# Row- and column-tiled matmuls and one list schedule for all engines, in a kernel of memory-recurrent attention and a SwiGLU layer

## The chip, the cores and the metric

One core of one Trainium2 chip. The metric is the device time of one execution in microseconds (us); several runs were taken of each kernel that is compared closely. Runs carry a state: "fast" if they lie within 1.5% of the fastest of the same kernel; a single run is "unknown".

## The reference

```python
def _A_ref(x, mem0, Wq, Wk, Wv, Wo, seg_len):        # x: 2048 x 576, 32 heads of 128, 8 memory rows
    mask = (idx[:, None] < M) | (idx[:, None] >= idx[None, :])
    mem = mem0
    for s in range(n_seg):                           # 64 segments of 32 rows, one after the other
        h = jnp.concatenate([mem, xs], axis=1)       # 40 rows
        q, k, v = ...                                # three einsums of h with Wq, Wk, Wv
        p = _softmax(where(mask, q k^T * scale, -1e9))
        o = einsum('bhte,hed->btd', p v, Wo)
        mem = o[:, :M, :].copy()                     # the recurrence
        outs.append(o[:, M:, :])
# _B_ref: (silu(x w1) * (x w3)) w2 with 4608 inner columns; everything bf16
x = x + _A_ref(_layernorm(x), ...);  x = x + _B_ref(_layernorm(x), ...)
x = x + _A_ref(_layernorm(x), ...);  x = x + _B_ref(_layernorm(x), ...)   # the same weights
```

Cut: the random inputs, the batch dimension of 1. The model width of 576 is 4.5 times 128, and 9 times 64; this is what the change turns on.

## The kernel before

72 steps. In step t, layer 1 handles segment t and layer 2 segment t - 8, side by side as 2 x 40 columns. Steps 8 to 63 hold both layers, the first and last eight steps one. Four steps share one FFN job (128 rows of each layer that has some); jobs 0, 1, 16 and 17 hold one entry, the others two. All matmuls of Q, K and V contract over 128 rows in five passes, where the fifth holds the last 64 rows of Wq or Wv in one half and those of Wk (or of the other half of Wv) in the other, and meets zeros in the half that it doesn't use:

```python
for kind in range(2):                                    # Q, then K
    accv = acc[:, 0:hg * 2 * QW]...
    Wm, tailc = (WQ, 4) if kind == 0 else (WK, 5)
    for hl in range(hg):                                 # 6 or 4 heads
        for c in range(4):
            mm(accv[:, hl], lhsT=Wm[:, c, hh * E:(hh + 1) * E], rhs=ht_cols(c), ...)      # 128 x 128 weights, 80 columns
        mm(accv[:, hl], lhsT=T1[:, hh * E:(hh + 1) * E], rhs=ht_cols(tailc), ...)
    nc.scalar.activation(QKT[...], acc..., ACT.Copy)     # all Q/K copies on ScalarE
...
for c in range(4):                                       # V: HT is the stationary operand, 512 columns of Wv stream
    mm(acc[0:104, 0:a1 - a0], lhsT=HTt[:, c, :], rhs=WV[:, c, a0:a1], ...)
...
for gu, tailc in ((0, 4), (1, 5)):                       # FFN up: w1, then w3
    for c in range(4):
        mm(accv[:, gu, lo:hi], lhsT=W13M[:, wss[gu], c, fb * P:(fb + 1) * P], rhs=XTB[:, c, lo:hi], ...)
    mm(accv[:, gu, lo:hi], lhsT=W13T[:, wt, fb * P:(fb + 1) * P], rhs=XTB[:, tailc, lo:hi], ...)
```

The order of the work is fixed by hand: slots within a step, rings of buffers. Cut: softmax, output projection, layernorm, FFN down.

## Time and profile before

| kernel before | |
|---|---|
| time, first three runs | 3563.51 us (3555.35 to 3567.45) |
| TensorE / VectorE / ScalarE busy | 93% / 54% / 46% |
| matmuls, with a weight load each | 58,470 |
| one step in the middle (steps 12 to 63) | 50.1 us |

The prediction shows the page's main lines, the stages and a stretch of the timeline. Two lines that it did not show turn out to matter. The first is of the table of DMA queues (queue and kind: packets, MB, share of the 16 engines):

```profile
q8 instruction: 458, 7.50, 0.9%
```

I take queue 8 for the one that brings TensorE's own program: it has 458 packets of 16,384 bytes. The page counts 58,470 matmuls and as many weight loads; their sum divided by 458 packets is 255 (256 in the kernel after, with 725 packets), so my estimate from these counts is that a packet holds 256 instructions of 64 bytes. At 0.9% of the DMA engines it looks negligible. The second is a window, the first 60 us of the kernel before, in which the attention weights load (columns as in the stage table of the prediction):

```profile
0.00:60.00 60.00, 18.87 (x246) 15.73 (x246) 13.87 (x39) 8.23 (x15) 11.38 (x20) 0.83 1.06 336
```

### The profile page before, as it was taken

To read this page: it belongs to the slowest core of one execution; us is meant where nothing else is said; L and a number is where in the kernel's file an instruction comes from. 1 tells how busy PE (TensorE), PEld (TensorE's weight loads), DVE (VectorE), ACT (ScalarE), POOL (GpSimd) and SP (SyncE) were. 2 spreads that over 40 slices of the span, in tenths; PEclk is the share of its full clock that TensorE was granted. 3 is DMA by queue.
4 is the path that set the end of the run, shared out by engine and by line. 5 is a ranking of instruction groups with operands and counts; after the bars stand their busy time and mean duration, and the time that the engine had idled before them with its cause. 6 is when DMAs were issued, how large, how long until landed. Compare 5 with 4: busy or idle time off the path is not lost.

```text
span 3562.8 us, 131473 instructions
## 1 busy us (share of the span) xinstructions
PE 3323.7 (93%) x58470; PEld 2801.4 (79%) x58470; DVE 1916.3 (54%) x5614; ACT 1621.3 (46%) x3865; POOL 61.8 (2%) x109
## 2 busy tenths in 40 slices
PE   5999999999999999999999999999999999999996
PEld 4888877877787778878787878878787878888785
DVE  3455555555555555555555555555555555555553
ACT  2544544444444444444444444444444444444441
POOL 1000000000000000000000000000000000000000
PEclk8999999999999999999999999999999999999997
DMA  8033323223222322323222322323222323223236
GB/s 256 3 95 89 102 82 95 76 73 102 74 84 69 97 87 82 89 74 96 76 82 72 101 86 82 88 74 96 77 84 73 102 77 92 83 71 96 78 114 183
DMA packets 504617, 321.65 MB, mean 90 GB/s; under 512 B 31081, under 2 KB 501361, under 8 KB 504049
## 3 DMA queue, kind: packets, MB, share of 16 engines
q1 hardware_dynamic: 500976, 306.17, 29.5%
q8 instruction: 458, 7.50, 0.9%
q0 software_dynamic: 3072, 7.08, 0.6%
q14 instruction: 111, 0.90, 0.1%
HBM read 308.42 MB, written 2.36 MB: 87 GB/s over the span
## 4 chain that ended last, share of the span: by engine, by line
PE 64%; issue 18%; DMA 8%; DVE 6%; ACT 2%; POOL 1%; SPq 0%; POOLq 0%; DVEq 0%; ACTq 0%
PE bank L174 62%; DMA W13M<-in_B_w_dram 7%; PE bank L177 2%; POOL LNS L239 1%; DVE TT L534 1%; DVE XR L491 1%; DMA T<-in_A_Wq_dram 1%; DVE LNS L233 1%; DVE LNS L234 1%; DVE HTT L535 1%; DVE XN L240 1%; DVE XR L548 0%; DVE PB L405 0%; DVE STAT L402 0%; ACT TT L533 0%
## 5 line engine op out<-in xcount | busy, mean ns | idle before, releaser
L174 PE MATMUL bank<-HT,T 128*128 128x80 bf16 x4608 | 847.0, 204 | 3.9 <-DVE HT L276 3.9
L174 PE MATMUL bank<-XTB,W13M 128*128 128x256 bf16 (+1 forms) x5184 | 695.6, 263 | 88.7 <-DMA W13M<-in_B_w_dram 80.2
L174 PE MATMUL bank<-WV,HT 128*104 128x512 bf16 (+1 forms) x2880 | 629.7, 341 | 1.7 <-ACT QKT L355 1.0
L355 ACT ACTIVATE QKT<-bank 128x480 bf16<-128x480 f32 (+1 forms) x864 | 452.2, 524 | 374.2 <-PE bank L174 325.8
L533 ACT ACTIVATE TT<-bank 128x256 bf16<-128x256 f32 (+1 forms) x648 | 233.6, 360 | 826.5 <-PE bank L174 826.3
L174 PEld LDWEIGHTS <-W13M 128*128 128x128 bf16 x5184 | 450.9, 99 | 172.7 <-DMA W13M<-in_B_w_dram 107.3
L174 PEld LDWEIGHTS <-HT 128*104 128x104 bf16 x3600 | 411.3, 128 | 191.4 <-DMA T<-in_A_Wv_dram 14.7
L174 PE MATMUL bank<-HT,WQ 128*128 128x80 bf16 x9216 | 494.5, 204 | 41.1 <-ACT HT L471 22.2
L174 PE MATMUL bank<-OT,WO 128*128 128x80 bf16 x11520 | 516.1, 202 | 12.3 <-ACT OT L429 12.1
L174 PEld LDWEIGHTS <-WO 128*128 128x128 bf16 x11520 | 473.6, 100 | 43.0 <-issue 14.2
L174 PEld LDWEIGHTS <-WQ 128*128 128x128 bf16 x9216 | 439.8, 101 | 65.5 <-issue 46.2
L174 PE MATMUL bank<-HT,WK 128*128 128x80 bf16 x9216 | 484.8, 204 | 1.4 <-DVE HT L278 1.2
L174 PEld LDWEIGHTS <-T 128*128 128x128 bf16 x4608 | 466.4, 101 | 0.6
L174 PEld LDWEIGHTS <-WK 128*128 128x128 bf16 x9216 | 437.6, 101 | 3.1 <-DVE HT L278 2.1
L534 DVE SCALAR_TENSOR_TENSOR TT<-TT,bank 128x256 bf16<-128x256 bf16 (+1 forms) x648 | 250.7, 387 | 348.3 <-ACT TT L533 346.0
L174 PE MATMUL bank<-W2C,HTT 128*128 128x288 bf16 x2284 | 349.2, 288 | 18.1 <-DVE HTT L535 10.7
L395 DVE TENSOR_TENSOR SME<-bank,maskb 104x240 f32<-104x240 f32 (+1 forms) x432 | 162.3, 376 | 351.1 <-PE bank L174 350.3
L183 DVE CAST VG<-bank 104x256 bf16<-104x256 f32 x288 | 122.1, 424 | 424.4 <-ACT VG L181 225.9
L174 PE MATMUL bank<-XTB,W13T 128*128 128x256 bf16 (+1 forms) x1296 | 338.3, 263 | 0.0
L181 ACT ACTIVATE VG<-bank 104x512 bf16<-104x512 f32 x432 | 257.7, 597 | 169.1 <-PE bank L174 160.5
L548 DVE SCALAR_TENSOR_TENSOR XR<-bank,XR 128x288 f32<-128x288 f32 x576 | 259.3, 455 | 112.1 <-PE bank L174 105.5
L174 PEld LDWEIGHTS <-HTT 128*128 128x128 bf16 x2304 | 215.0, 98 | 83.4 <-issue 20.0
(67 smaller groups left out, 3400.9 us busy)
## 6 DMA issues: line engine op xcount, KB each, us to landing
W13M<-in_B_w_dram SPq DMA_DIRECT2D x648, 256.0 KB, 3.0
W2C<-in_B_w_dram SPq DMA_DIRECT2D x319, 288.0 KB, 3.2
W13T<-in_B_w_dram SPq DMA_DIRECT2D x648, 32.0 KB, 2.6
XR<-in_A_x_dram POOLq DMA_DIRECT2D x16, 288.0 KB, 4.8
WO<-in_A_Wo_dram SPq DMA_DIRECT2D x1, 4608.0 KB, 20.6
WQ<-in_A_Wq_dram SPq DMA_DIRECT2D x4, 768.0 KB, 9.8
WK<-in_A_Wk_dram SPq DMA_DIRECT2D x4, 768.0 KB, 12.9
WV<-in_A_Wv_dram SPq DMA_DIRECT2D x4, 768.0 KB, 13.7
```

Source lines behind the costliest of these rows:

```text
L174: return _chain(nc.tensor.matmul(*a, **k))
L177: return _chain(nc.tensor.transpose(*a, **k))
L181: nc.scalar.activation(out_ap, in_ap, ACT.Copy)
L183: nc.vector.tensor_copy(out_ap, in_ap)
L233: nc.vector.bn_stats(st[:, 0, :], X[:, 0:288])
L234: nc.vector.bn_stats(st[:, 1, :], X[:, 288:576])
L239: nc.gpsimd.tensor_tensor(rstd, ve, mhalf[:], op=ALU.pow)
L355: nc.scalar.activation(QKT[:, qs, kind, 0:hg, :], acc[:, 0:hg * 2 * QW].rearrange("p (b n) -> p b n", b=hg), ACT.Copy)
L395: nc.vector.tensor_tensor(sme, Sps[0:104, 0:hg, :], maskb[0:104, :].unsqueeze(1).to_broadcast([104, hg, QW]), op=ALU.add)
L533: nc.scalar.activation(tt, GAv, ACT.Tanh, scale=0.5)
L534: nc.vector.scalar_tensor_tensor(tt, tt, 1.0, GAv, op0=ALU.add, op1=ALU.mult)
L548: nc.vector.scalar_tensor_tensor(Xs, yp[:, 0:288], 0.5, Xs, op0=ALU.mult, op1=ALU.add)
```

## The change

The intent: no pass of TensorE over zeros, small matmuls side by side in separate tiles of the array, and an order of all engines that is computed by a list scheduler, whose model of TensorE charges 0.1 us for each change of tiling mode (0.095 us in the trace before, see the prediction).

- Q and K: Wq lies in partitions 0 to 63, Wk in 64 to 127, 9 chunks of 64 rows each. Two matmuls of 64 rows, one in each half of the array ("row pair"), are to run side by side in the place of one of 128. 288 pairs a step in place of 320 matmuls.
- V: eight tiles (2 row halves x 4 column strips), separately for the rows of x (which don't wait for the memory) and for the memory rows.
- P times V and FFN up in row pairs too; scores in two column tiles as before.
- PSUM as three double banks, one bank for scores, one for the output; in the tail, all FFN weights are loaded into the attention weights' space.
- Copies go to ScalarE or VectorE as the plan decides.

The core of the diff (cut: nearly everything, it rewrites the kernel):

```diff
-                for hl in range(hg):
-                    for c in range(4):
-                        mm(accv[:, hl], lhsT=Wm[:, c, hh * E:(hh + 1) * E], rhs=ht_cols(c),
-                                         start=(c == 0), stop=False)
-                    mm(accv[:, hl], lhsT=T1[:, hh * E:(hh + 1) * E], rhs=ht_cols(tailc),
-                                     start=False, stop=True)
+            for hl in range(4):
+                h0 = (4 * u + hl) * E
+                for c in range(NCH):                       # 9
+                    for r in (0, 1):                       # 0: Q, 1: K
+                        rr = slice(r * R64, (r + 1) * R64)
+                        self.mm(self.pair(pair)[:, r, hl * 2 * QW + q0:hl * 2 * QW + q1], self.T.WQK[rr, c, h0:h0 + E],
+                                HTt[rr, POS[c], q0:q1], c == 0, c == NCH - 1, tile_position=(r * R64, 0))
...
+            for c in range(NCH):                           # V of the x rows
+                for r in (0, 1):
+                    for p0, li, q in todo:                 # four column strips
+                        self.mm(self.pair(pair)[p0:p0 + SEG, r, :], HTt[rr, POS[c], XO[li]:XO[li] + SEG],
+                                T.WV[rr, c, q * 512:(q + 1) * 512], ..., tile_position=(r * R64, p0))
...
-            wdma(Wt[:, :, c0:c1], wd[0:4 * P, c0:c1].rearrange("(c p) n -> p c n", p=P))
+            for r, wd in ((0, self.a.wq), (R64, self.a.wk)):
+                self.dma(self.T.WQK[r:r + R64, :, c0:c1], wd[:, c0:c1].rearrange("(c p) n -> p c n", p=R64))
...
+        if e == "PE":
+            key = lambda x: x[1].prio + (mode_pen if x[1].mode != mode else 0.0)
...
+            if n.mode != mode:
+                dur += SWITCH                              # 0.1
+                mode = n.mode
```

## The prediction

> **What bounds the kernel now.** I read the page first, then a table of stages, then groups of instructions, then one stretch of the timeline.
>
> ```profile
> PE 3323.7 (93%) x58470; PEld 2801.4 (79%) x58470; DVE 1916.3 (54%) x5614; ACT 1621.3 (46%) x3865; POOL 61.8 (2%) x109
> PEclk8999999999999999999999999999999999999997
> PE 64%; issue 18%; DMA 8%; DVE 6%; ACT 2%; POOL 1%; SPq 0%; POOLq 0%; DVEq 0%; ACTq 0%
> ```
>
> TensorE (PE) is busy 93% at nearly full clock and makes up most of the chain that ended last ("issue" there is TensorE following itself too). VectorE and ScalarE are half idle. So I count TensorE's time. The table of stages (us; busy time of each engine with its instructions; clock, DMA share, GB/s):
>
> ```profile
> core 0: us, PE busy (x) PEld busy (x) DVE busy (x) ACT busy (x) POOL busy (x), PEclk, DMA share, GB/s
> 0.00:80.00 80.00, 38.06 (x664) 32.71 (x665) 22.92 (x67) 18.87 (x40) 11.38 (x20) 0.87 0.92 285
> 80.00:177.00 97.00, 94.12 (x1904) 81.56 (x1901) 46.00 (x134) 51.17 (x116) 0.00 (x0) 1.00 0.01 3
> 177.00:345.00 168.00, 158.48 (x2979) 137.03 (x2977) 88.25 (x283) 78.58 (x191) 1.65 (x3) 1.00 0.34 97
> 1729.00:1928.00 199.00, 191.49 (x3332) 160.68 (x3330) 111.68 (x322) 93.42 (x224) 3.40 (x6) 0.99 0.29 85
> 3319.00:3484.00 165.00, 156.00 (x2958) 135.23 (x2956) 84.03 (x269) 78.19 (x189) 1.13 (x2) 1.00 0.33 98
> 3484.00:3563.00 79.00, 47.46 (x443) 36.73 (x443) 28.66 (x98) 11.71 (x39) 1.14 (x2) 0.76 0.62 185
> ```
>
> The ends of the stages are starts of the 72 YTS evictions, one per step. The program is 72 steps (64 segments, the second layer 8 later). Steps 8 to 63 hold both layers, 0 to 7 and 64 to 71 one. Four steps share one FFN job. Start and tail are limited by DMA (0.92 and 0.62 of the engines); the middle takes 50.1 us a step (721 to 2927 us, 44 steps). One-layer steps still take 32 us without an FFN, 41 with one.
>
> A matmul's mean duration (204 ns at 80 columns) contains its latency; the cost is the distance between starts:
>
> ```profile
> 1800.40 1.04 PE L174 MATMUL bank<-WV,HT 128*104 128x512 bf16 x4
> 1801.28 0.38 PE L174 MATMUL bank<-T,HT 128*104 128x512 bf16 x1
> 1801.50 0.60 PE L174 MATMUL bank<-WV,HT 128*104 128x256 bf16 x4
> 1801.93 0.27 PE L174 MATMUL bank<-T,HT 128*104 128x256 bf16 x1
> 1802.05 1.24 PE L174 MATMUL bank<-OT,WO 128*128 128x80 bf16 x30
> 1803.12 0.60 PE L174 MATMUL bank<-XTB,W13M 128*128 128x256 bf16 x4
> 1803.56 0.27 PE L174 MATMUL bank<-XTB,W13T 128*128 128x256 bf16 x1
> 1804.10 0.27 PE L174 MATMUL bank<-XTB,W13T 128*128 128x256 bf16 x1
> 1804.30 0.33 PE L174 MATMUL bank<-QKT 128*64 128x40 bf16 x11
> ```
>
> 30 Wo matmuls take 1803.12 - 1802.05 = 1.07 us: **36 ns** at N=80. Medians of all starts: 109 ns at 256, 122 at 288, 215.5 at 512, 56 at 128. From the last FFN matmul (1804.10) to the first, column-tiled, score (1804.30) are 0.20 us in place of 0.109: a **mode switch costs some 0.095 us**. Inside the scores the two column tiles run side by side: instruction by instruction, the 40-column tile starts every 25 ns and the 64-column tile every 32, so a pair costs 32 ns, not the sum 57.
>
> [...]
>
> **The change, part by part**, per two-layer step, before -> after, us of TensorE:
> - Q and K: 32 heads x 2 x 5 = 320 matmuls x 36 = 11.5 -> 32 x 9 row pairs = 288 x 36 = 10.4. D = 576 is 4.5 times 128; the zero-padded fifth pass becomes half a pass.
> - V: 8 blocks of 512 x 5 x 215.5 = 8.6 -> x rows 2 x 9 rounds of eight tiles (two row, four column), memory rows 1 x 9: 27 x 216 = 5.8. The rounds that hold x rows need no memory and may run ahead of the recurrence.
> - Scores 1.1 -> 1.0; P transposes 1.0 -> 32 x 46 (N=104) = 1.5; PV 32 x 36 = 1.15 -> the same in pairs; Wo 160 x 36 = 5.8, unchanged.
> - Output transposes 10 x 56 = 0.55 -> 10 per four steps = 0.14; layernorm transposes 0.25 -> 0.2.
> - FFN up: 360 x 109 / 4 = 9.8 -> 324 x 109 / 4 = 8.8. FFN down 144 x 122 / 4 = 4.4, unchanged.
>
> Sum: 44.1 -> 39.2. The measured 50.1 less 44.1 leaves 6.0: some 1.5 for about 16 switches, the rest waits. After, about 42 groups in four modes (8 QK, 3 V, 4 each of scores, transposes, PV, Wo, 4.5 FFN up, 9 down); if the scheduler pairs them, some 21 switches, 2.0 us. For waits I take 2.8 of the former 4.5, because all engines follow one plan whose durations (PSUM copy 0.07 + n x 0.000833 us on ScalarE) agree with the trace (0.467 us between starts at 480). **44 us** a step.
>
> One-layer steps win more: N falls from 80 to 40 columns and one x round of V serves both column sets. QK 288 x 25 = 7.2, V 18 x 216 = 3.9, scores 0.8, transposes 1.5, PV 0.8, Wo 160 x 25 = 4.0: 18.2 against 30 before. The chain QK, softmax, PV, Wo, memory columns then shows: eleven VectorE and ScalarE instructions per group, at 0.3 to 0.5 us. I estimate 23 us a step without FFN, 28 with a one-entry FFN (324 x 56 + 72 x 122 over 4 steps: 6.7), 36 with a two-entry one, 37 for two layers with a one-entry FFN.
>
> Stages, us: load and step 0, 78 (the same 19 MB of weights through the same DMA: 80 before); steps 1-3, 70 (97); 4-7, 112 (168); 8-11, 148 (171); 12-63, 52 x 44 = 2288 (2607); 64-67, 144 (196); 68-71, 112 (165); tail 52 (79: 15.9 MB of FFN weights at the opening's 285 GB/s is 56 us, part of it loaded earlier into the dead attention weights). Sum **3004 us**; I say 3000, 16% less.
>
> VectorE and ScalarE: the W2 additions double (two FFN blocks accumulate in PSUM instead of four), everything else is a little less in bigger pieces. Groups of instructions that I scaled:
>
> ```profile
> L355 ACT ACTIVATE QKT<-bank 128x320 bf16<-128x320 f32 x288 | 124.4, 432 | 22.0 <-PE bank L174 14.1 <-ACT PTS L420 0.7
> L534 DVE SCALAR_TENSOR_TENSOR TT<-TT,bank 128x256 bf16<-128x256 bf16 x504 | 209.9, 416 | 264.4 <-ACT TT L533 262.6
> L548 DVE SCALAR_TENSOR_TENSOR XR<-bank,XR 128x288 f32<-128x288 f32 x576 | 259.3, 455 | 112.1 <-PE bank L174 105.5
> ```
>
> Per step QK copies 16 x 0.43, V 6 x 0.6, P and O 8 x 0.7, the rest of softmax 14, FFN 4.5 x 3.5, layernorm and sundry 5: near 51 us on two engines, under 60% of 2 x 44. They should not bind on average.
>
> **Rivals.**
> 1. *Row pairs do not overlap.* Two 128-column weight loads per 36 ns have never been seen here: 128 columns in 36 ns is the most the trace shows. At 54 ns a pair QK costs 5.2 us more a step: 3370 us. Wholly serial (72 ns, FFN up doubled too): over 4000, slower. For it: no row tile in this trace. Against: column tiles pace independently[...]. Chance 10%. The same for eight tiles of V at 216 ns: if they took twice that, the saving on V turns into a loss of 3 us and the whole into 3400 us.
> 2. *PSUM becomes the bound.* Three double banks serve QK, V, PV, FFN and layernorm, one bank scores and P transposes. I add up 65 us of holding per step over three pairs, 22 of 44: no bound on average, but an order fixed beforehand stalls when a copy comes late. 3 us more a step: 3190 us. Chance 20%.
> 3. *The plan is better than I think* and waits fall to 1 us a step: 2900 us. Chance 20%.
>
> **Range and chances.** 2850 to 3220 holds rival 3 and most of 2. Slower needs serial row pairs: 4%; within 2%: 3%; faster: 93%.
>
> **What would show it.** Start-to-start of QK pairs 36 ns (N=80), 25 (N=40), FFN pairs 109, V rounds 216; 42 to 46 us between YTS evictions in the middle, 21 to 25 in steps 1-3; TensorE still over 90% busy with VectorE under 70%; the tail DMA-limited, 45 to 60 us. Wrong if pairs take over 45 ns, if TensorE idles over 10% of the middle waiting for copies, or if VectorE heads the chain.

## The result, and the profile after

| | before | after |
|---|---|---|
| time, median of four fast runs each | 3559.43 us | **3465.06 us** (3458.90 to 3475.82) |
| ratio | | 0.974 (0.972 to 0.976) |

Ratios here are the mean time of one kernel's fast runs over that of the other's fast runs of the same rounds, so not quite the ratio of the medians. The change is 2.6% faster; 16% were predicted, and the result lies 245 us above the top of the range.

The page of the kernel after, the same lines as before:

```profile
PE 2949.1 (85%) x92853; PEld 2414.3 (70%) x92853; DVE 2242.8 (65%) x4915; ACT 1207.7 (35%) x2607; POOL 65.3 (2%) x108
PEclk8789999999999999999999999999999999999898
q8 instruction: 725, 11.88, 1.5%
PE 63%; DVE 17%; issue 11%; ACT 5%; SPq 2%; DMA 1%; POOL 0%; POOLq 0%; ACTq 0%; DVEq 0%
```

TensorE's busy time fell by 375 us, and its share fell too, to 85%: it stands still more than before. No other engine took over; VectorE has 65%. The number of matmuls rose by 59%, and with it the instruction packets, from 458 to 725. The stages (us, from the ends of steps):

| | step 0 | 1-3 | 4-7 | 8-11 | 12-63 | 64-67 | 68-71 | tail |
|---|---|---|---|---|---|---|---|---|
| before | 79.5 | 97.0 | 168.0 | 171.6 | 2606.6 | 196.6 | 164.8 | 78.8 |
| predicted | 78 | 70 | 112 | 148 | 2288 | 144 | 112 | 52 |
| after | 101.9 | 97.7 | 157.1 | 177.9 | 2511.9 | 177.3 | 168.8 | 64.3 |

The loss against the prediction is in every stage: 24 us in step 0, 224 in the middle, 193 in the one-layer and mixed steps together, 12 in the tail. Steps 1 to 3 are the starkest: the largest relative gain was expected (28%) and none came. Windows of the kernel after: the first 60 us, steps 1 to 3, steps 12 to 63, the tail:

```profile
0.00:60.00 60.00, 19.54 (x522) 11.95 (x522) 14.83 (x34) 6.21 (x12) 6.18 (x14) 0.93 1.06 219
102.00:199.60 97.60, 74.81 (x3032) 59.98 (x3033) 43.04 (x122) 30.23 (x88) 0.56 (x1) 0.81 0.02 4
534.60:3046.50 2511.90, 2242.65 (x68517) 1846.34 (x68509) 1742.62 (x3725) 938.16 (x1932) 48.85 (x77) 0.99 0.39 89
3392.60:3457.00 64.40, 40.54 (x731) 30.65 (x730) 30.96 (x62) 9.06 (x22) 1.15 (x2) 0.79 0.88 188
```

In steps 1 to 3 no engine is near its limit: TensorE 77%, VectorE 44%, ScalarE 31%, DMA 2%. (The lower clock there, 0.81, goes with a TensorE that stops often: the same stage has 0.91 and 0.96 in two experiments below in which it stops less.) In the first 60 us the DMA engines are as full as before, but move 219 GB/s where they moved 336.

What TensorE waits for is in the group of Q/K matmuls and in the table of waits (us, times, longest; the line counts all matmuls that write one of the three double banks, most of them Q/K):

```profile
L467 PE MATMUL pair<-HT,WQK 64*128 64x80 bf16 (+1 forms) x41472 | 812.7, 195 | 265.9 <-issue 226.1
```

```profile
PE pair L467 <- issue: 263.0, 229, 4.7
```

It has idle time of 266 us ahead of Q/K matmuls, and most of it is "issue": no semaphore, no buffer, no transfer of data that the profile shows. A stretch of the timeline shows such a stop inside a run of Q/K matmuls (start, length, group):

```profile
1746.19 1.47 PE L467 MATMUL pair<-HT,WQK 64*128 64x80 bf16 x72
1747.60 0.66 PE L467 MATMUL pair<-W2C,HTT 128*128 128x288 bf16 x4
1748.52 1.63 PE L467 MATMUL pair<-W2C,HTT 128*128 128x288 bf16 x12 [0.26 <-DVE HTT L473]
1750.08 3.97 PE L467 MATMUL pair<-HT,WQK 64*128 64x80 bf16 x212
1755.98 0.25 PE L467 MATMUL pair<-HT,WQK 64*128 64x80 bf16 x4 [1.93 <-issue]
```

212 matmuls start 17.9 ns apart, then nothing for 1.93 us, then the last four of the same run. 212 matmuls with their weight loads are 424 instructions. The records of queue 8 have one packet ending at 1749.60 and the next at 1754.69; TensorE goes on 1.29 us after the end of the second. (The two start 5.3 us apart, so the spacing is not a fixed rate; I take the smallest one for the bound of the supply.)

So I went through the records of queue 8 and of TensorE together, which the tables of the profile don't do:

- In the whole kernel after, packets **never start less than 3.26 us apart** (5% of the intervals are under 3.46, the median is 4.17). A packet takes 0.9 to 1.4 us. Where TensorE had stopped, it went on 1.27 to 1.59 us (10 to 90%) after the end of a packet. The minimum is the same in steps 1 to 3 (3.44 us), where data transfers are 4 GB/s: other transfers don't cause it.
- 256 instructions per 3.3 us is **13 ns an instruction**, 26 ns for a weight load with its matmul.
- I counted TensorE's started instructions against the packets. Taking the moments at which TensorE stood still as zero, the number in hand when a new packet starts is at most 287, with a median of 175. From this I estimate that some two packets' worth is all there is (287 and the 256 on their way are 543), and that the next fetch starts when about one is left. In the kernel before, with the same zero, it was 158 to 291 at every packet start, median 247: it never ran dry. Its packets start 7.2 us apart in the median.
- Gaps of over 0.25 us between two Q/K matmuls of one run: 205 of them, 282 us in all. Where they fall ties them to the packets: if one counts all of TensorE's instructions that started before each gap, 191 of the 205 counts (264 of the 282 us) leave the same remainder, 193, when divided by 256. TensorE stops after whole packets.

The cadences within the runs, start to start where nothing stops them (medians over four pairs, for V over one round, for the transposes of P from one start to the next):

| | predicted | measured after |
|---|---|---|
| Q/K pair, 80 columns | 36 ns | 35.8 |
| Q/K pair, 40 columns | 25 | 25.3 |
| FFN pair, 256 columns | 109 | 109 |
| V round of eight tiles, 512 columns | 216 | 216 |
| P transpose, 104 columns | 46 | 46 |

A Q/K pair has four instructions, so at 35.8 ns it asks for one each 8.9 ns, and at 25.3 for one each 6.3. The supply gives at best one in 13.

### The profile page after: what moved, and what is told of

Its sections match the earlier page's. It is cut to its first block, busy times and chain, and to the rows that moved or that the text cites. A ratio compares the mean times of both kernels' runs of the same rounds, so it can differ in the third digit from the quotient of the medians.

```text
span 3456.9 us, 196772 instructions
## 1 busy us (share of the span) xinstructions
PE 2949.1 (85%) x92853; PEld 2414.3 (70%) x92853; DVE 2242.8 (65%) x4915; ACT 1207.7 (35%) x2607; POOL 65.3 (2%) x108
## 4 chain that ended last, share of the span: by engine, by line
PE 63%; DVE 17%; issue 11%; ACT 5%; SPq 2%; DMA 1%; POOL 0%; POOLq 0%; ACTq 0%; DVEq 0%
PE pair L467 51%; PE YB L467 7%; PE SB L467 5%; DVE HTT L473 4%; DVE STAT L473 3%; DVE PB L473 3%; DVE SME L473 3%; SPq L476 2%; DVE XR L473 1%; ACT HT L470 1%; ACT SME L470 1%; DMA W<-in_B_w_dram 1%; DVE VX L473 1%; DVE HT L473 1%; DVE LNS L473 1%
## 5 line engine op out<-in xcount | busy, mean ns | idle before, releaser
L467 PE MATMUL pair<-HT,WQK 64*128 64x80 bf16 (+1 forms) x41472 | 812.7, 195 | 265.9 <-issue 226.1
L467 PEld LDWEIGHTS <-WQK 64*128 64x128 bf16 x42048 | 771.6, 97 | 337.2 <-issue 307.2
L467 PE MATMUL pair<-XTB,W 64*128 64x256 bf16 (+1 forms) x11016 | 610.0, 262 | 30.2 <-issue 11.4
L467 PEld LDWEIGHTS <-W 64*128 64x128 bf16 x11016 | 505.1, 95 | 89.5 <-issue 44.8
L470 ACT ACTIVATE QKT<-pair 128x320 bf16<-128x320 f32 (+1 forms) x790 | 301.4, 407 | 735.9 <-PE pair L467 703.2
L467 PE MATMUL pair<-WV,HT 64*32 64x512 bf16 (+1 forms) x14400 | 453.0, 390 | 52.8 <-DVE HT L473 15.4
L467 PE MATMUL YB<-OT,WO 128*128 128x80 bf16 (+1 forms) x11520 | 443.4, 198 | 21.0 <-issue 11.6
L473 DVE SCALAR_TENSOR_TENSOR XR<-pair,XR 128x576 f32<-128x576 f32 x576 | 416.9, 752 | 27.2 <-PE pair L467 17.9
L467 PE MATMUL pair<-W2C,HTT 128*128 128x288 bf16 x2232 | 347.9, 290 | 21.3 <-DVE HTT L473 12.5
L473 DVE TENSOR_TENSOR PB<-SME,STAT 40x256 bf16<-40x256 f32 (+1 forms) x1024 | 321.9, 319 | 20.5
L473 DVE CAST VX<-pair 128x512 bf16<-128x512 f32 x128 | 88.5, 692 | 210.6 <-ACT VX L470 210.6
```

The lines of the kernel that those rows point to most:

```text
L467: self.ch("PE", self.nc.tensor.matmul(out, lhsT=lhsT, rhs=rhs, start=start, stop=stop, skip_group_check=True, **k))
L470: self.ch("ACT", self.nc.scalar.activation(*a, **k))
L473: self.ch("DVE", getattr(self.nc.vector, fn_)(*a, **k))
```

## The experiments

The supply of instructions is theory A. The other letters in the texts stand for rivals, each tested by the experiment that it was made for: D, that the opening lacks transfers side by side; E, that the plan's durations for VectorE are off; F, that the shape of the weight transfers slows the opening. All kernels but one gave a result that was accepted as correct. That needs a caution: four compute wrong queries or keys on purpose (told below), and three of these passed nevertheless; the fourth, which was told wrong, has wrong values (V) as well. So wrong queries and keys move the output too little for the tolerance. The comparison doesn't vouch for the Q/K part of any kernel here.

### Half the instructions for Q and K

One weight load serves two heads' columns (the input repeated: 160 columns in place of 80). Same columns through the array, half the instructions, wrong numbers.

```diff
-            for hl in range(4):
+            for hl in (0, 2):
...
-                        self.mm(self.pair(pair)[:, r, hl * 2 * QW + q0:hl * 2 * QW + q1], self.T.WQK[rr, c, h0:h0 + E],
-                                HTt[rr, POS[c], q0:q1], c == 0, c == NCH - 1, tile_position=(r * R64, 0))
+                        out = self.pair(pair)[:, r, hl * 2 * QW:(hl + 2) * 2 * QW].rearrange("p (h n) -> p h n", h=2)
+                        self.mm(out[:, :, q0:q1], self.T.WQK[rr, c, h0:h0 + E],
+                                HTt[rr, POS[c], q0:q1].unsqueeze(1).to_broadcast([R64, 2, q1 - q0]), ...)
```

> Wrong result on purpose: in the Q and K projection each row-tiled matmul streams twice the columns (the same 80 twice, 160) and serves two heads, so TensorE streams as long as before (69 ns for a pair instead of 2 x 36) with half the matmuls: 41,472 -> 20,736, TensorE's instructions 185.7k -> 144k. Theory A (TensorE's instructions come in packets of 256, never less than 3.3 us apart, so long runs of 17.8 ns matmuls starve): the idle time inside Q/K runs, 262 us in the changed kernel, falls under 60 us and the time to 3120-3230 us. Rival B (TensorE waits for copies out of PSUM, because three double banks are too few and VectorE is 65% busy): the copies are the same, so at most 50 us are gained, 3410-3470 us.

Measured: 3167.56 us, one run, 298 less than the change. The plan and all other work are untouched. Two lines of the page of this kernel, then one of its waits:

```profile
q8 instruction: 563, 9.22, 1.3%
L467 PE MATMUL pair<-HT,WQK 64*128 64x160 bf16 (+1 forms) x20736 | 716.6, 224 | 59.3 <-issue 12.8
```

```profile
PE pair L467 <- issue: 31.5, 35, 2.7
```

The waits for "issue" fell from 263 us to 31.5, the gaps inside Q/K runs from 282 to 37. The middle takes 45.0 us a step, next to the predicted 44; steps 1 to 3 take 73.7 us, predicted 70. Not all of the 298 us is supply: a matmul at 160 columns also streams a little quicker than two at 80 (69.2 ns a pair against 2 x 35.8), and in one-layer steps 35.8 replaces 2 x 25.3. From the trace that is some 34 us for the 16 one-layer steps and 19 for the rest. About **245 us** are left for the supply, and the gaps inside Q/K runs fell by as much.

### Q and K on 128 rows again

Nearly all the rest of the change stays. 320 matmuls of 128 rows replace the 288 pairs, so TensorE streams more columns and needs fewer instructions (640 in place of 1152 a step). To make room, the statistics of the softmax have one field and the mask is bf16. The layout also makes Wq and Wk load into 128 partitions at a time, which shortens step 0 (84.2 us against 101.9; see the opening, below).

```diff
-                for c in range(NCH):
-                    for r in (0, 1):
-                        self.mm(..., self.T.WQK[rr, c, h0:h0 + E], HTt[rr, POS[c], q0:q1], ..., tile_position=(r * R64, 0))
+            for kind in (0, 1):
+                for hl in range(4):
+                    for c in range(5):
+                        w = self.T.WQK[:, 4 * kind + c if c < 4 else 8, h0:h0 + E]
+                        p = c if c < 4 else (9, 4)[kind]
+                        self.mm(self.pair(pair)[:, kind, ...], w, HTt[:, p, q0:q1], c == 0, c == 4)
```

> Right result. Undoes one part: Q and K projections on all 128 rows again, 5 passes per head and matrix (320 matmuls a step) instead of 9 row pairs (576), all else as in the changed kernel. Theory A: TensorE's instructions 185.7k -> 149k, no idle time of over 0.25 us without a semaphore inside Q/K runs, which outweighs 75 us more of streaming (11.5 against 10.4 us a step): 3180-3300 us, faster than both kernels. Rival B (copies out of PSUM): 75 us more streaming show in full, 3500-3560 us. Rival C (the row tiling is worth its cadence as I predicted): as B.

Measured: 3259.76 us (3255.74 to 3263.56, four runs), ratio to before 0.917 (0.914 to 0.919), against 0.974 for the change. Undoing the very part that was to save TensorE time makes the kernel 205 us faster, 18 of them in step 0. Two lines of its page, then one of its waits:

```profile
q8 instruction: 581, 9.52, 1.3%
L469 PE MATMUL pair<-HT,WQK 128*128 128x80 bf16 (+1 forms) x23040 | 837.8, 197 | 45.0 <-DVE VX L475 11.3
```

```profile
PE pair L469 <- issue: 25.7, 22, 3.1
```

One full-row matmul of 80 columns takes 36 ns and two instructions: 18 ns each, more than 13. It hardly runs dry: 25.7 us of "issue" in place of 263. The busy time at Q and K rises by 25 us, the stops of 226 us are gone.

### FFN up on 128 rows again

```diff
-                for c in range(NCH):
-                    for r in (0, 1):
-                        self.mm(..., W[rr, c, fb * P:(fb + 1) * P], self.T.XTB[rr, POS[c], lo:hi], ..., tile_position=(r * R64, 0))
+                for r in (0, 1):
+                    for c in range(5):
+                        w = W[:, 4 * r + c if c < 4 else 8, fb * P:(fb + 1) * P]
+                        self.mm(..., w, self.T.XTB[:, c if c < 4 else (9, 4)[r], lo:hi], c == 0, c == 4)
```

> Right result. Undoes another part alone: FFN up on all 128 rows, 360 matmuls of 109 ns per job instead of 648[...]. By streaming alone it costs 0.9 us a step more, 40-60 us in all: 3505-3525. Theory A expects part of that back: 10.4k fewer TensorE instructions (725 -> 684 packets) and slower matmuls let packets run ahead before Q/K, and W2 needs no change of mode after it (0.1 us for each of 324 units at most): 3400-3490 us, the idle time inside Q/K runs under 262 us but still over 150.

Measured: 3438.10 us (3437.50 to 3449.40, four runs), ratio 0.968 (0.965 to 0.970), 0.7% better than the change by the ratios, too little to be called faster. Packets 686; the gaps in Q/K runs fall from 282 to 195 us, although no Q/K instruction is touched:

```profile
PE pair L469 <- issue: 161.0, 161, 2.8
```

So a longer run of slow FFN matmuls ahead of Q/K seems to leave more in hand (not tested by itself). The FFN pairs themselves (109 ns for four instructions, 27 each) seldom run dry (21 us of gaps after whole packets in the change, see below), and their gain (60 us of busy time by the two pages) is more than taken back elsewhere: without them the middle is 24 us longer, but the other stages together are 45 us shorter, 15 of them in the tail. The FFN weights then load into 128 partitions too, so supply and loads are not separated here.

### Both together, and one buffer fewer

Q, K and FFN up on 128 rows, with three in place of four buffers for the copied Q/K (with four, this kernel does not build).

```diff
-    pools = {"pair": 3, "s": 1, "y": 1, "qkt": 4, ...
+    pools = {"pair": 3, "s": 1, "y": 1, "qkt": 3, ...
```

> Right result. Both Q/K and FFN up on 128 rows (one QKT buffer less, 3, to fit). Theory A: with Q/K undone little starvation is left (78 us), so undoing FFN up now costs its streaming (0.9 us a step, about 55 us) and wins back some changes of mode (up to 30 us) and part of the 78: 3250-3310 us, same or slower than qk_full's 3260. If instead FFN's pairs cost more than their cadence for another reason, it is faster than qk_full by over 20 us as it was by itself (3438 against 3465).

Measured: 3261.95 us (3255.10 to 3267.61), ratio 0.917. As expected, the same as with Q/K alone. But the stages say that two things cancel: the middle is 51 us longer (2490.5 against 2439.4), the one-layer steps 4 to 7 and 68 to 71 and the tail are 46 us shorter. This led to the mixture below.

### Row pairs for Q and K put into the kernel before

The opposite test: only this part of the change, in the old kernel. Wrong numbers (weights and inputs lie in the old layout).

```diff
+            accs = [accA.take(), accA.take()]
+            for hl in range(hg):
+                for c in range(9):
+                    for kind, Wm in ((0, WQ), (1, WK)):
+                        mm(accv[:, hl], lhsT=Wm[rr, c % 4, hh * E:(hh + 1) * E], rhs=rhs, ..., tile_position=(64 * kind, 0))
```

> Wrong result on purpose. One part of the change alone, put into the kernel before: Q and K projections as nine row pairs a head (rows 0-63 stream for Q, 64-127 for K, into two banks; the rows are not laid out for it, so the numbers are wrong, the stream of instructions is right). 320 -> 576 matmuls a step, TensorE's instructions 116.9k -> 153.8k. By cadence alone Q and K take 10.4 instead of 11.5 us a step, -79 us, and some 6 more changes of mode a step, +43 us: 3500-3570 us. Theory A (instruction packets at least 3.3 us apart): idle time inside Q/K runs appears, 100 us or more, and the time is 3620-3850 us.

Measured: 3798.87 us, one run. The time is in the range expected, but **for another reason than I gave**. Packets rise to 602, but only some 2 us of stops follow a packet. The Q/K pairs run at 35.8 ns. Instead, both banks of the old ring are held by one group of Q/K, so V waits for ScalarE's copy (the wait below, 75 us; nothing like it stands at the top of the old kernel's waits), and the time lost at changes of mode rises from 171 to 272 us.

```profile
PE bank L174 <- ACT QKT L356: 75.0, 99, 2.7
```

This says more about theory A than the expectation did: Q/K comes there in portions of at most 108 matmuls between slow V and output matmuls, and does not starve. Those are 216 instructions; in the stop shown above, TensorE starved after 424. So the supply binds over a stretch of one or two packets, not in the average.

### A plan that knows the supply

The scheduler gets a stock of 256 instructions, refilled at 3.35 us per 256, puts dense groups off when the stock is low, and plans a group longer when the stock can't feed it (that line is cut from the diff).

```diff
+SUPPLY = 3.35 / 256
+            have = min(CAP, credit + (t - seen) / SUPPLY)
+            key = lambda x: old(x) + 0.3 * max(0.0, count(x[1]) - have - x[1].dur / SUPPLY) * SUPPLY
```

> Right result, the changed kernel's instructions, only their order differs: the plan counts TensorE's instructions, 256 per 3.35 us with 256 in hand, and puts off dense work (Q/K, V) when the store is empty. Theory A, weak form (the starvation is a matter of order and can be hidden under slower matmuls): 3200-3330 us. Theory A, strong form (one and a bit packets in hand are fewer than one Q/K unit of 144 instructions plus its neighbours need, and Q/K heads the recurrence and cannot wait): 3400-3460 us.

Measured: 3513.99 us, one run: a miss, worse than the change. The stops in Q/K runs fell (282 to 209 us), those after a packet in all from 388 to 335, but TensorE waits more for VectorE (for its residual additions, FFN gate, V copies and softmax 117 us together, against 62 in the change). Q and K start the chain of each step, and in this run putting them off cost more than it saved. A better rule may exist; this one doesn't show the supply to be curable by order.

### VectorE's durations in the plan set to the measured ones

Theory E, in the variant with Q/K on 128 rows.

```diff
-            b = node("DVE", 2 * dve(256 * ne), em.ffn_mul(ents, pair, htt), ...
+            b = node("DVE", 0.31 + 2 * dve(256 * ne) * 0.9, em.ffn_mul(ents, pair, htt), ...
-                e_ = node("DVE", dve(576), em.ffn_add(g, xr[g], pair), ...
+                e_ = node("DVE", 0.76, em.ffn_add(g, xr[g], pair), ...
```

> Right result. qk_full with the planned durations of two VectorE steps of the FFN set to the measured ones (W2 addition 0.665 -> 0.76 us, the two gate steps together 1.20 -> 1.39 us). Theory E: part of the 96 us that TensorE waits in qk_full for these two comes from a plan that thinks them shorter: 3225-3250 us. Rival (those waits come from the three PSUM pairs, whatever the order): 3255-3265 us.

Measured: 3262.99 us (3254.98 to 3267.32), ratio 0.917: no difference from 3259.76. Theory E falls.

### The opening: two queues

Theory D: Wq and Wk, and the halves of Wv, come through two queues at once.

```diff
-            for r, wd in ((0, self.a.wq), (R64, self.a.wk)):
-                self.dma(self.T.WQK[r:r + R64, :, c0:c1], ...)
+            self.dma(self.T.WQK[0:R64, :, c0:c1], ...)
+            self.dma2(self.T.WQK[R64:P, :, c0:c1], ...)       # ScalarE's queue
```

> Right result. Only the first loads of Wq/Wk and Wv change: the transfers into partitions 0-63 stay on SyncE's queue, those into 64-127 go to ScalarE's, so that both halves are written at the same time. Theory D (transfers into 64 partitions at a time move less per second): step 0 ends at 80-90 us instead of 102, the total falls by 12-22 us. Rival (the start is limited by bytes or by the supply of instructions to step 0): 98-104 us, total unchanged.

Measured: 3460.67 us, one run; step 0 takes 108.5 us in place of 101.9. Theory D falls in this form: two queues at once don't help. That transfers into 64 partitions move less per second, the text's other half, is what the next runs test.

### The opening: the shape of the transfers

Theory F: each transfer of Wq and Wk fills 128 partitions, with the same bytes per row (rows in the wrong place). Beside it, a control that still fills 64 partitions but takes the source's rows in another order, of Wv too (wrong as well, relative error 0.023).

```diff
-                self.dma(self.T.WQK[r:r + R64, :, c0:c1], wd[:, c0:c1].rearrange("(c p) n -> p c n", p=R64))
+                self.dma(self.T.WQK[:, 4 * i:4 * i + 4, c0:c1], wd[0:4 * P, c0:c1].rearrange("(c p) n -> p c n", p=P))
+                self.dma(self.T.WQK[i * R64:(i + 1) * R64, 8, c0:c1], wd[4 * P:D, c0:c1])
```

```diff
-                self.dma(self.T.WQK[r:r + R64, :, c0:c1], wd[:, c0:c1].rearrange("(c p) n -> p c n", p=R64))
+                self.dma(self.T.WQK[r:r + R64, :, c0:c1], wd[:, c0:c1].rearrange("(p c) n -> p c n", p=R64))
```

> Wrong result on purpose: in the changed kernel only the first loads of Wq and Wk differ, each transfer fills 128 partitions with 4 chunks (and a tail of 64) in place of 64 partitions with 9, the bytes are the same; the weights lie in the wrong rows. Theory F (the 64 x 9 shape of the transfer, not the number of TensorE's instructions, makes the opening slow): step 0 ends at 83-92 us instead of 102, DMA over 250 GB/s in the first 60 us instead of 219, the total falls by 10-20 us. Rival (qk_full's early 84 us came from its fewer instructions in step 0): 98-104 us.

> Wrong result on purpose: the same transfers into 64 partitions, 9 KB to each, but partition p takes rows 9p to 9p+8 of the weights instead of rows p, p+64, ... Theory F1 (the order of the addresses in memory is at fault): step 0 ends at 83-92 us. Theory F2 (writing 64 partitions is at fault, whatever is read): 98-104 us as in the changed kernel.

Measured, one run each: 3441.68 and 3454.71 us; step 0 takes **88.5** and 100.9 us (101.9 after, 79.5 before). The first 60 us of the wide loads, then of the control:

```profile
0.00:60.00 60.00, 19.79 (x585) 12.95 (x587) 16.69 (x39) 7.48 (x15) 6.17 (x14) 0.93 1.06 261
```

```profile
0.00:60.00 60.00, 18.87 (x522) 11.77 (x522) 15.02 (x35) 6.22 (x12) 6.17 (x14) 0.92 1.07 221
```

261 GB/s against 221. A 1024-byte packet takes 59 ns (median) with wide loads, 85 in the control and in the change, 51 in the kernel before. So it is the shape with 64 partitions (85 ns in both orders), not the order of addresses. Wv still loads into 64 partitions in the wide variant, which may be one reason why it doesn't reach the 336 GB/s of the kernel before (not tested by itself). With two halves of 64 partitions in turn in one queue, the first 60 us of the change show 219. The FFN's 512-byte packets show the same: on average 39.1 ns each in the change, 28.6 where FFN up is on 128 rows, 28.3 before.

### A mixture

Q/K on 128 rows; FFN up on 128 rows in jobs with one entry, in row pairs with two; three Q/K buffers.

```diff
-            ff = node("PE", 20 * mm, em.ffn_up(...), ..., mode="full",
+            ff = node("PE", (20 if ne == 1 else 18) * mm, em.ffn_up(...), ..., mode="full" if ne == 1 else "row",
```

> Right result. Q/K on 128 rows everywhere, FFN up on 128 rows only in jobs with one entry (steps 4 to 11, 68 to 71 and the tail) and as row pairs in jobs with two (steps 12 to 67). From the stages of qk_full (steps 4-7 132 us, 68-71 143, tail 65.5, middle 2439) and qkff_full (118, 126, 50, middle 2491): 3260 - 14 - 17 - 15 = 3205-3230 us if stages add up and Q/K stays fed in the middle. If the middle's 2439 needed the fourth QKT buffer, which does not fit here: 3240-3290 us.

Measured: **3176.16 us** (3175.88 to 3176.83, four runs), ratio to before **0.894** (0.893 to 0.896), better than expected and the best kernel here that is meant to compute the right thing. Its page:

```profile
PE 2954.5 (93%) x73269; PEld 2451.8 (77%) x73269; DVE 2252.7 (71%) x4939; ACT 1190.8 (38%) x2585; POOL 65.6 (2%) x108
PE 51%; DVE 36%; ACT 5%; issue 4%; SPq 1%; DMA 1%; POOL 1%; POOLq 0%; DVEq 0%; ACTq 0%
```

TensorE has the same busy time as in the change, 2954 us against 2949, but 93% of the span: what the mixture gains is stops.

### Three Q/K buffers alone

The mixture's middle (2395.2 us) is better than that of Q/K on 128 rows (2439.4), which differs from it there by the number of buffers (and by the place of the FFN's input in memory).

```diff
-             "qkt": 4,     # in the variant with Q/K on 128 rows
+             "qkt": 3,
```

> Right result. qk_full with three QKT buffers instead of four, nothing else. The hybrid's middle (steps 12-63) took 2395 us against qk_full's 2439 though both do the same work there; they differ in this buffer and in what the plan made of it. If the buffer (Q/K may run less far ahead, so its dense stretches are shorter) is the reason: middle 2385-2410 us, total 3205-3230. If not: 2430-2450 and 3250-3270.

Measured: 3233.19 us (3232.12 to 3238.02), ratio 0.910, 3 us above the range; middle 2396.3 us, inside its range. So fewer buffers gain the middle's 43 us. Whether the buffer itself or the other order that the plan makes of it does so isn't separated; the plan's own end moves from 2970 to 2941 us with it. With this run the FFN's row pairs can be judged at three buffers throughout: two-entry jobs in pairs shorten the middle by 95 us (2490.5 with all on 128 rows, 2395.2 in the mixture), one-entry jobs in pairs lengthen the rest by 57 (3233 against 3176 us; the tail is 74.1 against 50.1). A pair at 128 columns takes 56 ns for four instructions, 14 each, just above the supply's 13, and its weights load into 64 partitions; which of the two counts is not separated.

The stages of the main variants:

| | step 0 | 1-3 | 4-7 | 8-11 | 12-63 | 64-67 | 68-71 | tail |
|---|---|---|---|---|---|---|---|---|
| half the Q/K instructions | 102.7 | 73.7 | 131.0 | 156.4 | 2340.4 | 153.8 | 135.9 | 71.6 |
| Q/K on 128 rows | 84.2 | 76.0 | 132.4 | 160.0 | 2439.4 | 156.9 | 143.1 | 65.5 |
| mixture | 84.9 | 82.3 | 118.7 | 156.7 | 2395.2 | 156.8 | 129.3 | 50.1 |

## Why the prediction was wrong

**The step that failed is the sum.** The prediction took each kind of matmul's cadence, multiplied by the count, and added switches and waits to "44 us a step". It named TensorE's array, PSUM, VectorE, ScalarE and the DMA of weights as what could bind, and left out what a matmul needs before any of them: its instruction. The change buys columns with instructions (2635 a step in the middle, by 68,517 matmuls and as many loads over 52 steps). The average would allow it: 2635 x 13 ns is 34 us of a 48 us step. But Q and K ask for 1152 of them at 8.9 ns each. An estimate from these numbers: 1152 x 13 ns less 288 x 35.8 ns is 4.7 us a step, if they ran in one stretch with nothing in hand; measured are 282 us / 72 = 3.9.

How the 453 us between the sum of the predicted stages (3004) and the span (3457) divide:
- **Supply of instructions to Q and K: about 245 us**, shown by halving the instructions and, from the other side, by Q/K on 128 rows.
- **Opening: 24 us.** The prediction wrote "the same 19 MB of weights through the same DMA". The bytes are the same; the shape isn't. 13 us of it came back with wide loads for Wq and Wk.
- **Tail: 12 us** over the 52 predicted. FFN weights on 128 rows bring it to 50.1 in the mixture.
- **The rest, some 170 us.** With half the Q/K instructions, 117 us are still left between step 0 and the tail, 52 of them in the middle (45.0 in place of 44 us a step); another 53 that kernel made good by streaming less, as worked out above. Gaps of over 0.25 us that fall after whole packets, by the remainder above, come in the change to 20 us within V, 19 within scores, 21 within FFN up and 15 within the output projection, 75 in all. With half the Q/K instructions some 60 us of such gaps remain in the whole kernel, so perhaps half of the 117 is supply again. None of this was tested by itself, and the cause of the remainder stays open.

**What was right.** Row pairs overlap fully (35.8 ns; rival 1 at 10% did not come). That they would was the author's estimate: the trace before had column tiles side by side (25 and 32 ns) and no row tile. Eight tiles of V run at once, at the 216 ns that were predicted. N of 40 gives 25.3 ns a pair, so the one-layer steps could have had their gain: with half the instructions, steps 1 to 3 fell to 73.7 us, against 70 predicted and 97 before. VectorE does not bind (65%). The direction was right, and faster by over 2%.

**The rivals.** Rival 2 (PSUM) is not the cause: halving the instructions moved more than half of the loss without touching a PSUM buffer, the waits for semaphores at Q/K matmuls come to 40 of 266 us, and the stops fall after whole packets, which no copy out of PSUM would arrange. Rival 3 (fewer waits) did not come. A fourth rival was missing, and the page had its line: queue 8.

**The signs.** "Wrong if pairs take over 45 ns" did fire: the mean Q/K pair, stops included, takes 47.4 ns (983.9 us start to start over 20,736 pairs). But the mean hid that the clean cadence was right, and the reason that rival 1 gives for slow pairs, weight loads that don't overlap, was wrong (35.8 ns for two loads with their matmuls). "Idles over 10% of the middle waiting for copies": it idles 10.7% (2242.65 us busy of 2511.9), mostly not for copies. Three more signs failed: TensorE is 85% busy and not over 90%, a step in the middle takes 48.3 us and not 42 to 46, the tail 64.3 and not 45 to 60.

The scheduler in the kernel makes the same mistake: its own clock ends at 2889 us for the change and at 2970 for Q/K on 128 rows, so it ranks the two the wrong way round. Hardware took 3465 and 3260.

## What to carry to other kernels

Before tiles make matmuls smaller, divide the time of each dense stretch by its instructions, counting the weight loads: here the limit was 13 ns an instruction, sustained, with an estimated two packets of 256 in hand. Row pairs at 80 columns (8.9 ns) lost on it (282 us of gaps), full-row matmuls (18 ns) and FFN pairs at 256 columns (27 ns) hardly did (25.7 us of "issue", 21 us of gaps). With 59% more matmuls, a saving of 375 us of TensorE's busy time came to 94 us of time. And a layout made for the array also sets the shape of the loads: in the opening, two halves of 64 partitions came at 219 GB/s, where the kernel before had 336.
